# Dilated and sliding window attention with a gated unit: a half-pair order, loads by two pairs, and a ring for y

## The chip, the cores and the metric

One core of a Trainium2 chip runs the whole program. The time is the device time of the core in microseconds (us), from several executions; beside the timed runs there is one profiled execution, whose trace gives every other time here. TensorE (PE in the profile, PEld for its weight loads) multiplies matrices, VectorE (DVE) and ScalarE (ACT) do the elementwise work, GpSimd (POOL) converts inputs, SyncE (SP) issues the loads.

## The reference

For 8 batches, 8 heads, 576 positions and a head dimension of 64, attention is computed under a causal mask: heads 0 to 3 see the last 32 positions ("plain" here), heads 4 to 7 every fourth of the last 128 ("dilated"). The result, with the heads side by side as 512 channels, goes through a gated unit: a causal depthwise convolution of five taps gives the gate, a matrix gives the value, and a second matrix the output.

```python
scores = scale * np.matmul(q, k.transpose(0, 1, 3, 2))
rel = pos[:, None] - pos[None, :]
mask_plain = (rel >= 0) & (rel < window)                       # window = 32
mask_dil = (rel >= 0) & (rel < window * dilation) & (rel % dilation == 0)   # dilation = 4
...
attn = np.exp(scores); attn = attn / (np.sum(attn, axis=-1, keepdims=True) + 1e-09)
x = np.matmul(attn, v)                                          # heads side by side: (B, S, 512)
...
for k in range(K):                                              # K = 5
    gate_pre += conv_w[k][None, None, :] * xp[:, k:k + S, :]
gate = 1.0 / (1.0 + np.exp(-gate_pre))
return gate * (x @ w_val) @ w_out
```

## The kernel before, in words

**Pairs.** The work goes by head pairs: four pairs for each of eight batches, 32 in all, listed in `order` (L82). In batch 0 the dilated pairs come first; later batches go plain, dilated, plain, dilated. Positions are grouped by their remainder modulo 4, so that a dilated head becomes four heads with an ordinary window of 32 over 144 positions (96 and a rest of 48).

**One pair.** `load_qk` and `load_v` (L89, L106) issue the loads of a pair on SP, two pairs ahead in program order; four buffers of each input let them run ahead. `convert` (L132) casts on POOL: V of a dilated pair, or q and k of a plain pair (96 rows and 48 rows apart, four casts). `transpose_in` (L152) transposes q and k on TensorE into a PSUM bank; VectorE copies them to `qT` and `kT` (L182), except `kT` of a plain pair, which ScalarE copies (L179). A plain pair has four transposes of 96 rows and four of 48 for each of q and k; a dilated one six of 96.

`scores(i, hf)` (L187) does one half of the pair: matmuls into a PSUM tile `sc`, exp on ScalarE into `et` (L212), and the mask as a multiplication on VectorE (L219). `attn_v(i, hf)` (L222) multiplies the masked `et` by V and a column of ones, into the same `sc` tile; VectorE takes the reciprocal of the sums (`rec`, L251) and scales the rest into `xn` (L256). The pool `ps_s` has two such tiles (L60), so a tile is taken again two halves later, once its `xn` is done. `transpose_x` (L261) transposes `xn` on TensorE, for a dilated pair by turns of 96 and 48 rows (L269, L271), and ScalarE copies the result into `xT` (L278), the 512 channels by position.

**The gated unit.** Tokens are cut into ten groups (L283). A group has, for each block of 128 channels, a conv unit (L297: five diagonal matmuls, tanh on ScalarE) and a val unit (L310: four matmuls, then VectorE combines gate and value into `y_all`, L320), and an out unit for each 128 tokens (L326: four matmuls, a ScalarE copy to `osb`, L332, and the store, issued on ScalarE's queue, L333). Banks for these and for the transposes come from one pool of four (L61).

**The order.** Every engine works in the order in which the program emits instructions. The main loop (L447) emits, for pair i: the loads and casts of pair i+2; both scores with exp and mask; `fill`; `attn_v(i, 0)`; the input transposes of pair i+1; `attn_v(i, 1)`; `fill`; `transpose_x(i)`. `fill` (L432) takes units from a queue while a budget lasts, 3.2 a pair in two shares; a conv costs 1.1, a val or out 0.9. A group enters the queue when its last batch's attention is done; so batch 0 has no units beside it, batches 1 to 6 have twelve each (the group of the batch before), and what the last batch leaves is done at the end (L472): 1024 tokens' worth, in groups of 448, 320 and 256.

The weights are loaded through POOL's queue in pairs 0 and 2 (L454, L456); the diagonal matrices of the convolution are made on VectorE after each of the first four pairs (L401).

Of the kernel before, what the change touches and what calls it, by code (L numbers as in the profile page):

```python
# [24 lines left out]
def kernel(  # L25
# [30 lines left out]
    inbuf = ctx.enter_context(tc.tile_pool(name="inbuf", bufs=4))  # L56
# [10 lines left out]
    NKT_, NVP, NVD, NET = 3, 3, 2, 4  # L67
    kTs = [consts.tile([128, 640], BF16, name=f"kT{i}") for i in range(NKT_)]
    ets = [consts.tile([128, 2, 384], BF16, name=f"et{i}") for i in range(NET)]
    vps = [consts.tile([128, NT, 2, D + 1], FP32, name=f"vp{i}") for i in range(NVP)]  # L70
# [3 lines left out]
    y_all = consts.tile([128, NCH, NTOK], BF16, name="y_all")  # L74
# [7 lines left out]
    order = [(b, g) for b in range(B) for g in ((2, 3, 0, 1) if b == 0 else (0, 2, 1, 3))]  # L82
    nat = {}
    cnt = {"p": 0, "d": 0}
# [4 lines left out]
    def load_qk(i):  # L89
        b, g = order[i]  # L90
        t = {}
        for name, src in (("q", q), ("k", k)):
            rows = src[b, 2 * g:2 * g + 2].rearrange("h (p r) d -> p h (r d)", r=R)
            a = inbuf.tile([P0, 2, R * D], FP32, name=f"{name}a")
            nc.sync.dma_start(out=a, in_=rows[0:P0])
            if is_dil(i):
                z = inbuf.tile([2 * P1, R * D], FP32, name=f"{name}zd")
                for hh in range(2):
                    nc.sync.dma_start(out=z[hh * P1:(hh + 1) * P1], in_=rows[P0:TT, hh, :])
            else:  # L100
                z = inbuf.tile([P1, 2, R * D], FP32, name=f"{name}zp")
                nc.sync.dma_start(out=z, in_=rows[P0:TT])
            t[name] = (a, z)
        nat[i] = t

    def load_v(i):  # L106
        b, g = order[i]
        t = nat[i]
        if g >= NG // 2:
            rows = v[b, 2 * g:2 * g + 2].rearrange("h (p r) d -> p h (r d)", r=R)  # L110
            a = inbuf.tile([96, 2, R * D], FP32, name="va")
            nc.sync.dma_start(out=a, in_=rows[0:96])
            z = inbuf.tile([80, 2, R * D], FP32, name="vz")
            nc.sync.dma_start(out=z, in_=rows[64:144])
            j = cnt["d"] % NVD
            cnt["d"] += 1
            t["v"] = (a, z, vd0[j], vd1[j])
        else:
            vt = vps[cnt["p"] % NVP]
            cnt["p"] += 1  # L120
            vv = v[b, 2 * g:2 * g + 2]
            nc.sync.dma_start(out=vt[:, 0, :, 0:D],
                              in_=vv[:, 0:128, :].rearrange("h p d -> p h d"))
            for hh in range(2):
                nc.sync.dma_start(
                    out=vt[:, 1:NT, hh, 0:D],
                    in_=bass.AP(tensor=v.tensor,
                                offset=v.offset + ((b * H + 2 * g + hh) * S + 64) * D,
                                ap=[[D, 128], [96 * D, NT - 1], [1, D]]))
            t["v"] = (vt,)  # L130

    def convert(i):  # L132
        if is_dil(i):
            a, z, c0, c1 = nat[i]["v"]
            for src, dst in ((a, c0), (z, c1)):
                nc.gpsimd.tensor_copy(  # L136
                    dst[:, :, :, 0:D], src.rearrange("p h (r d) -> p h r d", r=R))
        else:
            for name in ("q", "k"):
                res = []  # L140
                for src, n, x in zip(nat[i][name], (P0, P1), "az"):
                    c = work.tile([n, R, 2, D], BF16, name=f"{name}c{x}")
                    nc.gpsimd.tensor_copy(
                        c.rearrange("p r h d -> p h r d"),
                        src.rearrange("p h (r d) -> p h r d", r=R))
                    res.append(c)
                nat[i][name] = tuple(res)
# [4 lines left out]
    def transpose_in(i, name):  # L152
        a, z = nat[i][name]
        ps = bank(BF16)
        if is_dil(i):
            av, zv = hi_bf16(a), hi_bf16(z)
            pv = ps[:, 0:S].rearrange("p (f h t) -> p f h t", f=2, h=2)
            for f in range(2):
                cols = slice(f * 128, f * 128 + 128)
                for hh in range(2):  # L160
                    nc.tensor.transpose(out=pv[:, f, hh, 0:P0], in_=av[:, hh, cols],
                                        identity=ident_b[0:P0, 0:P0])
                nc.tensor.transpose(out=pv[:, f, :, P0:TT], in_=zv[:, cols],  # L163
                                    identity=ident_b[0:2 * P1, 0:2 * P1])
        else:
            for r in range(R):
                nc.tensor.transpose(out=ps[:, r * TT:r * TT + P0],
                                    in_=a[:, r, :, :].rearrange("p h d -> p (h d)"),
                                    identity=ident_b[0:P0, 0:P0])
            for r in range(R):  # L170
                nc.tensor.transpose(out=ps[:, r * TT + P0:(r + 1) * TT],  # L171
                                    in_=z[:, r, :, :].rearrange("p h d -> p (h d)"),
                                    identity=ident_b[0:P1, 0:P1])
        if name == "k":
            dst = kTs[i % NKT_]
        else:
            dst = work.tile([128, S], BF16, name="qT")
        if name == "k" and not is_dil(i):
            nc.scalar.copy(out=dst[:, 0:S].rearrange("p (t r) -> p t r", r=R),  # L179
                           in_=ps[:, 0:S].rearrange("p (r t) -> p t r", r=R))  # L180
        else:
            nc.vector.tensor_copy(dst[:, 0:S], ps[:, 0:S])  # L182
        nat[i][name + "T"] = dst
# [3 lines left out]
    def scores(i, hf):  # L187
        b, g = order[i]
        dil = g >= NG // 2
        qT, kT = nat[i]["qT"], nat[i]["kT"]  # L190
# [8 lines left out]
        if dil:  # L199
            for hh in range(2):  # L200
                o = (2 * hf + hh) * TT
                mm(hh * 96, 96, kT[:, o:o + 128], qT[:, o:o + 96])
            for hh in range(2):
                o = (2 * hf + hh) * TT
                mm(192 + hh * 48, 48, kT[:, o + 64:o + 192], qT[:, o + 96:o + TT])
        else:
            for c in range(3):
                t = 3 * hf + c
                k0 = 0 if t == 0 else 96 * t - 32
                mm(c * 96, 96, kT[:, k0:k0 + 128], qr[:, :, 24 * t:24 * t + 24])  # L210
        et = ets[(2 * i + hf) % NET]
        nc.scalar.activation(out=et[:, :, 0:HALF], in_=ps[:, :, 0:HALF],  # L212
                             func=AF.Exp, scale=scale)
        ev = et[:, :, 0:HALF]
        if dil:
            for_mask = mask_d[:, None, :].to_broadcast([128, 2, HALF])
        else:
            for_mask = mask_p[:, hf:hf + 1, :].to_broadcast([128, 2, HALF])
        nc.vector.tensor_tensor(out=ev, in0=ev, in1=for_mask, op=ALU.mult)  # L219
        state[(i, hf)] = (ps, et)  # L220

    def attn_v(i, hf):  # L222
# [8 lines left out]
        for x in range(2):  # L231
            if dil:
                _, _, c0, c1 = nat[i]["v"]
# [9 lines left out]
            else:  # L243
                vb = hi_bf16(nat[i]["v"][0])
                for c in range(3):
                    nc.tensor.matmul(out=ps[:, x, c * DA:(c + 1) * DA],  # L246
                                     lhsT=et[:, x, c * 96:c * 96 + 128],
                                     rhs=vb[:, 3 * hf + c, x, :], start=True, stop=True)
# [12 lines left out]
    def transpose_x(i):  # L261
# [5 lines left out]
        if dil:  # L267
            for r in range(R):
                nc.tensor.transpose(out=pv[:, r, 0:96], in_=xn[:, 2 * r, :, :].rearrange("p h d -> p (h d)"),  # L269
                                    identity=ident_b[0:96, 0:96])  # L270
                nc.tensor.transpose(out=pv[:, r, 96:TT], in_=xn[0:48, 2 * r + 1, :, :].rearrange("p h d -> p (h d)"),  # L271
                                    identity=ident_b[0:48, 0:48])
        else:
            for t in range(NT):
                nc.tensor.transpose(out=pv[:, :, 24 * t:24 * t + 24], in_=xn[:, t, :, :].rearrange("p h d -> p (h d)"),
                                    identity=ident_b[0:96, 0:96])
# [3 lines left out]
        del nat[i]  # L280


    groups = [(512 * j, 512) for j in range(7)] + [(3584, 448), (4032, 320), (4352, 256)]  # L283
# [11 lines left out]
    gates = {}  # L295

# [13 lines left out]
    def val_unit(gi, c):  # L310
        t0, n = groups[gi]
        ps = bank()
        for o, col, ln in pieces(t0, n):
# [5 lines left out]
        gate = gates.pop((gi, c))  # L319
        nc.vector.scalar_tensor_tensor(  # L320
            out=y_all[:, c, t0:t0 + n], in0=gate[:, 0:n], scalar=1.0, in1=ps[:, 0:n],
# [4 lines left out]
    def out_unit(t0, n):  # L326
        ps = bank()
        for c in range(NCH):
            nc.tensor.matmul(out=ps[0:n, :], lhsT=y_all[:, c, t0:t0 + n],  # L329
# [6 lines left out]
    load_qk(0)  # L336
    load_v(0)
# [22 lines left out]
    for x in kTs:  # L360
        nc.vector.memset(x[:, S:640], 0.0)
    for x in ets:
        nc.vector.memset(x[:, :, HALF:384], 1.0)
    for x in vps:
        nc.vector.memset(x[:, :, :, D:D + 1], 1.0 - 2.0 ** -9)
    convert(0)

    load_qk(1)
    load_v(1)
# [6 lines left out]
    band(mp[:, 0, 0, :, :], 0, [[1, R], [4, 24]], 1, W)  # L376
    band(mp[:, 1, 0, :, :], 32, [[1, R], [4, 24]], 1, W)
# [29 lines left out]
    COST = {"C": 1.1, "V": 0.9, "O": 0.9}  # L407
    done_tok = [0]

    def add_group(gi):  # L410
# [93 lines left out]
```

## Time and profile before

| | us |
|---|---|
| timed runs | 226.98, 231.23, 345.96 |
| median of the runs | 231.23 |
| the profiled execution's own time | 225.51 |
| its span, first to last instruction | 223.8 |
| TensorE busy | 189.1 |
| VectorE busy | 128.4 |
| ScalarE busy | 108.7 |
| GpSimd busy | 65.0 |
| first conv unit starts | 31.96 |
| last pair's attention ends, only gated units remain | 195.4 |

A line of a group or a timeline reads: source line, engine, operation, output <- input, partitions by elements. In a timeline the first column is the start in us from the beginning of the span, the second the duration; brackets hold the idle time before it, and what ended it. Matmuls are pipelined: the starts of consecutive ones are nearer than their durations, of which some 0.2 us is the way through the array. DMA moved 41.82 MB, 30.95 of them on SP's queue; 219 GB/s from 10 to 20 us, 225 and 227 in two steady batches.

### The profile page before, as it was taken

The numbers are of one execution on the slowest core, as the hardware profiler recorded it, in microseconds if no ns is written. First come the engines' busy times: TensorE is split into PE (matmuls) and PEld (weight loads), VectorE is DVE, ScalarE is ACT, GpSimd is POOL, SyncE is SP. The second block draws the span as 40 slices with busy tenths as digits, with TensorE's granted clock in tenths as the row PEclk, the third lists the DMA queues.
The fourth block names the chain that finished last, engine by engine and source line by source line (L and its number), as shares of the span: only waits on it lengthen the run. The fifth ranks groups of instructions, "written<-read, shape, count | busy, mean of one in ns | idle before, by whom it ended". The sixth has DMA issues, their size and how long they took to land.

```text
span 223.8 us, 5850 instructions
## 1 busy us (share of the span) xinstructions
PE 189.1 (85%) x2279; PEld 127.0 (57%) x2292; DVE 128.4 (57%) x311; ACT 108.7 (49%) x190; POOL 65.0 (29%) x123
## 2 busy tenths in 40 slices
PE   2666689878988898898898898889888988999992
PEld 0544545545655576556775686558655666454670
DVE  2566664775667556663666659656776566532320
ACT  2234444356554655475544753465536654643442
POOL 4296506420516150524146024602360200000000
PEclk9999999999999999996999999999999999999999
DMA  5799999747779799869989779778986300221232
GB/s 144 240 220 207 236 216 225 211 120 232 213 212 231 234 254 224 217 222 258 233 192 243 234 217 237 181 244 227 232 213 212 118 3 0 99 91 47 100 141 94
DMA packets 58757, 41.82 MB, mean 187 GB/s; under 512 B 29029, under 2 KB 54117, under 8 KB 58730
## 3 DMA queue, kind: packets, MB, share of 16 engines
q1 hardware_dynamic: 52480, 30.95, 56.1%
q10 hardware_dynamic: 5194, 9.45, 11.8%
q0 software_dynamic: 1056, 1.05, 2.9%
q8 instruction: 18, 0.29, 0.6%
q14 instruction: 9, 0.07, 0.1%
HBM read 33.04 MB, written 9.44 MB: 190 GB/s over the span
## 4 chain that ended last, share of the span: by engine, by line
PE 45%; DMA 15%; ACT 13%; DVE 10%; issue 7%; SPq 6%; ACTq 2%; POOL 0%; DVEq 0%
PE bank L303 16%; ACT et L212 9%; PE bank L315 8%; PE bank L329 5%; DVE et L219 4%; ACT osb L332 4%; DMA qa<-in_q_dram 4%; DVE xn L256 4%; DMA vp<-in_v_dram 3%; PE bank L269 3%; PE sc L246 2%; PE bank L271 2%; DMA ka<-in_k_dram 2%; ACTq L333 2%; DMA kzd<-in_k_dram 2%
## 5 line engine op out<-in xcount | busy, mean ns | idle before, releaser
L303 PE MATMUL bank<-xT,conv_diag 128*128 128x320 bf16 (+7 forms) x319 | 46.3, 295 | 0.3 <-DMA kzd<-in_k_dram 0.3
L256 DVE TENSOR_TENSOR xn<-sc,rec 96x512 bf16<-96x512 f32 (+1 forms) x64 | 39.7, 620 | 2.2
L212 ACT ACTIVATE et<-sc 128x576 bf16<-128x576 f32 x64 | 38.5, 660 | 4.8 <-PE sc L197 4.8
L307 ACT ACTIVATE gate<-bank 128x512 bf16<-128x512 f32 (+3 forms) x40 | 22.0, 556 | 32.8 <-PE bank L303 32.8
L315 PE MATMUL bank<-xT,w_val_b 128*128 128x320 bf16 (+7 forms) x254 | 37.1, 285 | 0.3 <-issue 0.3
L136 POOL CAST vda<-va 96x512 bf16<-96x512 f32 x16 | 10.0, 622 | 92.9 <-DMA va<-in_v_dram 79.3
L332 ACT ACTIVATE osb<-bank 128x512 f32<-128x512 f32 x36 | 21.6, 601 | 29.4 <-PE bank L329 23.4
L320 DVE SCALAR_TENSOR_TENSOR y_all<-gate,bank 128x512 bf16<-128x512 bf16 (+3 forms) x40 | 25.1, 628 | 18.0 <-PE bank L315 9.1
L303 PEld LDWEIGHTS <-conv_diag 128*128 128x128 bf16 x320 | 27.8, 100 | 12.6 <-issue 1.4
L329 PE MATMUL bank<-w_out_b,y_all 128*128 128x512 bf16 x134 | 33.7, 380 | 0.8 <-DVE y_all L320 0.2
L219 DVE TENSOR_TENSOR et<-et,mask_d 128x576 bf16<-128x576 bf16 x32 | 16.7, 524 | 27.9 <-ACT et L212 26.9
L278 ACT COPY xT<-bank 128x576 bf16<-128x576 bf16 x32 | 20.4, 637 | 23.1 <-PE bank L271 17.8
L219 DVE TENSOR_TENSOR et<-et,mask_p 128x576 bf16<-128x576 bf16 x32 | 16.8, 532 | 25.6 <-ACT et L212 24.6
L315 PEld LDWEIGHTS <-w_val_b 128*128 128x128 bf16 x256 | 20.8, 97 | 8.1
L329 PEld LDWEIGHTS <-y_all 128*128 128x128 bf16 x144 | 12.8, 98 | 14.4 <-DVE y_all L320 1.8
L179 ACT COPY kT<-bank 128x576 bf16<-128x576 bf16 x16 | 10.2, 638 | 20.4 <-PE bank L171 16.4
L236 PE MATMUL sc<-vda,et 96*128 96x65 bf16 x128 | 12.2, 203 | 7.6 <-DVE et L219 3.7
L246 PE MATMUL sc<-vp,et 128*128 128x65 bf16 x192 | 12.1, 201 | 7.5 <-DVE et L219 4.2
L269 PE MATMUL bank<-ident_b,xn 96*128 96x96 bf16 x64 | 14.1, 221 | 4.4 <-DVE xn L256 4.4
L251 DVE RECIPROCAL rec<-sc 96x8 f32<-96x8 f32 (+1 forms) x64 | 12.2, 191 | 9.5 <-PE sc L246 7.7
L182 DVE COPY qT<-bank 128x576 bf16<-128x576 bf16 x32 | 14.2, 444 | 3.3 <-PE bank L163 3.0
L236 PEld LDWEIGHTS <-et 96*128 96x128 bf16 x128 | 8.1, 100 | 14.1 <-DVE et L219 13.6
(62 smaller groups left out, 243.5 us busy)
## 6 DMA issues: line engine op xcount, KB each, us to landing
out_dram<-osb ACTq DMA_DIRECT2D x36, 256.0 KB, 2.3
qa<-in_q_dram SPq DMA_DIRECT2D x32, 192.0 KB, 4.1
ka<-in_k_dram SPq DMA_DIRECT2D x32, 192.0 KB, 3.4
vp<-in_v_dram SPq DMA_DIRECT2D x32, 160.0 KB, 3.8
va<-in_v_dram SPq DMA_DIRECT2D x16, 192.0 KB, 3.6
vz<-in_v_dram SPq DMA_DIRECT2D x16, 160.0 KB, 3.8
qzd<-in_q_dram SPq DMA_DIRECT2D x32, 48.0 KB, 3.4
kzd<-in_k_dram SPq DMA_DIRECT2D x32, 48.0 KB, 3.1
```

Of the source, the lines that this page charges most:

```text
L212: nc.scalar.activation(out=et[:, :, 0:HALF], in_=ps[:, :, 0:HALF], func=AF.Exp, scale=scale)
L219: nc.vector.tensor_tensor(out=ev, in0=ev, in1=for_mask, op=ALU.mult)
L236: nc.tensor.matmul(out=ps[:, x, hh * DA:(hh + 1) * DA], lhsT=et[0:96, x, hh * 96:hh * 96 + 128], rhs=c0[:, hh, r, :], start=True, stop=True)
L256: nc.vector.tensor_tensor(out=xo, in0=av[:, :, :, 0:D], in1=rec[:, :, 0:n, None].to_broadcast([96, 2, n, D]), op=ALU.mult)
L269: nc.tensor.transpose(out=pv[:, r, 0:96], in_=xn[:, 2 * r, :, :].rearrange("p h d -> p (h d)"), identity=ident_b[0:96, 0:96])
L278: nc.scalar.copy(out=xT[:, g, c0:c0 + S].rearrange("p (t r) -> p t r", r=R), in_=pv.rearrange("p r t -> p t r"))
L303: nc.tensor.matmul(out=ps[:, o:o + ln], lhsT=conv_diag[:, c, kk, :], rhs=xT[:, c, s:s + ln], start=(kk == 0), stop=(kk == K - 1))
L307: nc.scalar.activation(out=gate[:, 0:n], in_=ps[:, 0:n], func=AF.Tanh, scale=0.5)
L315: nc.tensor.matmul(out=ps[:, o:o + ln], lhsT=w_val_b[:, mc, c * 128:(c + 1) * 128], rhs=xT[:, mc, col:col + ln], start=(mc == 0), stop=(mc ...
L320: nc.vector.scalar_tensor_tensor(out=y_all[:, c, t0:t0 + n], in0=gate[:, 0:n], scalar=1.0, in1=ps[:, 0:n], op0=ALU.add, op1=ALU.mult)
L329: nc.tensor.matmul(out=ps[0:n, :], lhsT=y_all[:, c, t0:t0 + n], rhs=w_out_b[:, c, :], start=(c == 0), stop=(c == NCH - 1))
L332: nc.scalar.activation(out=osb[0:n, :], in_=ps[0:n, :], func=AF.Copy, scale=0.5)
```

## The change

The dilated pairs come first in every batch, and the loop runs by half pairs j = 0 to 63. Step j emits: at an even j the loads of two pairs (every second pair) and the casts of pair i+2; the scores and exp of half j+1; at an even j the output transposes of pair i-1 and the input transposes of pair i+1; `fill`; the mask of half j+1; `attn_v` of half j; `fill`. The pool of score tiles still has two.

Loads come by units of two pairs (four heads), with three buffers for q and k, two for the rest. The 48-row rests of q and k of a plain pair lie in one tile of 96 rows, so a plain pair has three casts and twelve input transposes of 96 rows; `kT` is then copied by ScalarE in two pieces. The dilated output transposes go four of 96, then four of 48. The first 32 columns of the plain keys are zeros, so that every key block starts at 96t. V of a plain unit is one load with one column of ones per block.

`fill` gets what is left of the planned units divided by the steps left, from step 9 on, split 0.6 and 0.4. The last three groups are 384, 384 and 256 tokens; what remains for the end are 640 tokens' worth. `y` is a ring of three tiles, one for each group.

```diff
-    inbuf = ctx.enter_context(tc.tile_pool(name="inbuf", bufs=4))
+    inbuf = ctx.enter_context(tc.tile_pool(name="inbuf", bufs=2))
...
+    units = [(b, d) for b in range(B) for d in (1, 0)]
+    order = [(b, 2 * d + e) for b, d in units for e in range(2)]
...
+    def load_unit(u, parts):
...
+            t[name] = inbuf.tile([P0, 4, R * D], FP32, name=f"{name}a", bufs=3)
...
+        for e in range(0, 2, step):
+            hl, hn = 2 * e, 2 * step
+            for n, (name, src) in enumerate((("q", q), ("k", k))):
+                rows = src[b, hs].rearrange("h (p r) d -> p h (r d)", r=R)
+                nc.sync.dma_start(out=t[name][:, hl:hl + hn], in_=rows[0:P0, hl:hl + hn])
...
     def convert(i):
...
+            for name in ("k", "q", "z"):
+                n = 2 * P1 if name == "z" else P0
+                c = work.tile([n, R, 2, D], BF16, name=f"{name}c")
...
+        for r in range(R):
+            o = r * TT + P0
+            step = S + r * P1 - o
+            pa = pq[:, o:o + P1]
+            dst = bass.AP(tensor=pa.tensor, offset=pa.offset,
+                          ap=[pa.ap[0], [step, 2], [1, P1]])
+            nc.tensor.transpose(out=dst, in_=flat(cz[:, r]), identity=ident)
+        nc.vector.tensor_copy(qT, pq[:, 0:S])
+        for lo, hi, src in ((0, P0, pk[:, 0:R * P0]), (P0, TT, pq[:, S:S + R * P1])):
+            nc.scalar.copy(
+                out=kT[:, R * lo:R * hi].rearrange("p (t r) -> p t r", r=R),
+                in_=src.rearrange("p (r t) -> p t r", r=R))
...
+    def masks(i, hf):
+        et = state[(i, hf)][1]
...
+        nc.vector.tensor_tensor(out=ev, in0=ev, in1=m, op=ALU.mult)
...
             for r in range(R):
-                nc.tensor.transpose(out=pv[:, r, 0:96], in_=xn[:, 2 * r, :, :].rearrange("p h d -> p (h d)"),
+                nc.tensor.transpose(out=pv[:, r, 0:96], in_=flat(xn[:, 2 * r]),
                                     identity=ident_b[0:96, 0:96])
-                nc.tensor.transpose(out=pv[:, r, 96:TT], in_=xn[0:48, 2 * r + 1, :, :].rearrange("p h d -> p (h d)"),
+            for r in range(R):
+                nc.tensor.transpose(out=pv[:, r, 96:TT], in_=flat(xn[0:48, 2 * r + 1]),
                                     identity=ident_b[0:48, 0:48])
...
-    groups = [(512 * j, 512) for j in range(7)] + [(3584, 448), (4032, 320), (4352, 256)]
+    groups = [(512 * j, 512) for j in range(7)] + [(3584, 384), (3968, 384), (4352, 256)]
...
+        if c == 0:
+            ys[gi] = moe_sb.tile([128, NCH, 512], BF16, name="y", bufs=3)
...
+    first_fill = 2 * NG + 1
+    left = [todo, 2 * n_steps - first_fill]
...
+    transpose_in(0)
+    scores(0, 0)
+    masks(0, 0)
+    for j in range(2 * n_steps):
+        i, hf = j // 2, j % 2
         b, g = order[i]
...
+        if hf == 0:
+            if i % 2 == 0 and i // 2 + 2 < len(units):
+                load_unit(i // 2 + 2, 1)
+            if i + 2 < n_steps:
+                convert(i + 2)
...
+        share = max(0.0, left[0]) / max(1, left[1]) if j >= first_fill else 0.0
...
+        if j + 1 < 2 * n_steps:
+            scores((j + 1) // 2, (j + 1) % 2)
+        if hf == 0:
+            if i > 0:
+                transpose_x(i - 1)
+            if i + 1 < n_steps:
+                transpose_in(i + 1)
+        fill(share * 0.6)
+        if hf == 0 and i > 0 and i % NG == 0:
+            queue.extend(ready_after.get(order[i - 1][0], []))
+        if j + 1 < 2 * n_steps:
+            masks((j + 1) // 2, (j + 1) % 2)
+        attn_v(i, hf)
+        fill(share * 0.4)
+        if hf == 1 and i < NCH:
+            conv_consts(i)
+    transpose_x(n_steps - 1)
+    queue.extend(ready_after[B - 1])
     while queue:
         run_item()
```

## The prediction

> **What bounds the kernel now.** I read the page first (engines, slices, chain of waits), then the windows by batch, then the timeline of one batch on TensorE, VectorE and ScalarE, then who waited for whom.
>
> ```profile
> span 223.8 us, 5850 instructions
> PE 189.1 (85%) x2279; PEld 127.0 (57%) x2292; DVE 128.4 (57%) x311; ACT 108.7 (49%) x190; POOL 65.0 (29%) x123
> ...
> PEclk9999999999999999996999999999999999999999
> ```
>
> TensorE leads with 85%, and one slice (from 100.7 us) shows a lower granted clock. The windows below are two steady batches (four head pairs each) and the tail; their columns are length, busy time and count of PE, PEld, DVE, ACT, POOL, then clock, DMA share, GB/s.
>
> ```profile
> 55.50:78.95 23.45, 20.95 (x286) 13.25 (x286) 14.85 (x34) 12.67 (x22) 8.30 (x13) 1.00 0.79 225
> 78.95:102.05 23.10, 20.92 (x285) 14.17 (x286) 14.31 (x34) 12.67 (x22) 8.39 (x15) 1.00 0.87 227
> 102.05:126.90 24.85, 22.68 (x285) 16.29 (x285) 14.98 (x34) 12.78 (x22) 8.98 (x15) 0.93 0.94 240
> ...
> 195.40:223.80 28.40, 23.82 (x146) 13.85 (x146) 7.35 (x15) 11.19 (x22) 0.00 (x0) 1.00 0.25 93
> ```
>
> A batch is 23.45 us; PE's 20.95 includes about 0.2 us of modelled drain per burst, so I count starts: the batch from 55.5 has gaps of 0.8, 1.1, 0.3, 1.1 and 0.7 us, 4 in all, and PE's own need is 19.4. So a batch is bound by PE, plus the places where PE catches up with VectorE or ScalarE:
>
> ```profile
> 86.82 0.24 PE L236 MATMUL sc<-vda,et 96*128 96x65 bf16 x2 [0.66 <-ACT et L212]
> ...
> 90.26 0.21 PE L269 MATMUL bank<-ident_b,xn 96*128 96x96 bf16 x1
> 90.40 0.19 PE L271 MATMUL bank<-ident_b,xn 48*128 48x48 bf16 x1
> 90.52 0.22 PE L269 MATMUL bank<-ident_b,xn 96*128 96x96 bf16 x1
> 90.67 0.19 PE L271 MATMUL bank<-ident_b,xn 48*128 48x48 bf16 x1
> ...
> 101.62 0.22 PE L269 MATMUL bank<-ident_b,xn 96*128 96x96 bf16 x1 [0.57 <-DVE xn L256]
> ```
>
> The reader sees the two stalls that the change aims at (attention times V waiting for the mask, transposes waiting for `xn`), and alternating heights at 0.13 us a transpose. VectorE in the same batch:
>
> ```profile
> 86.31 1.00 DVE L219 TENSOR_TENSOR et<-et,mask_d 128x576 bf16<-128x576 bf16 x2 [1.60 <-ACT et L212]
> 87.22 0.68 DVE L320 SCALAR_TENSOR_TENSOR y_all<-gate,bank 128x512 bf16<-128x512 bf16 x1
> 87.82 0.20 DVE L251 RECIPROCAL rec<-sc 96x8 f32<-96x8 f32 x1
> 88.05 0.69 DVE L256 TENSOR_TENSOR xn<-sc,rec 96x512 bf16<-96x512 f32 x1
> 88.66 0.44 DVE L182 COPY qT<-bank 128x576 bf16<-128x576 bf16 x1
> ```
>
> VectorE idles 1.5 to 2.1 us once per pair before the first mask, waiting for scores and exp; both halves share that wait.
>
> **The change on TensorE.** Plain input transposes fall from 16 to 12 and keep one height: four groups of heights took 63.62 to 64.59 = 0.97, twelve of 96 rows took 58.25 to 58.75 = 0.50 (the dilated ones). Grouped dilated output transposes: eight took 90.26 to 91.22 = 0.96; four of 96 then four of 48 took 63.62 to 64.11 = 0.49. Both save 0.47, two of each a batch: 1.9 us a batch, 15 us in eight if PE set the pace.
>
> **The change in the order.** The PSUM ring for scores keeps two buffers. Half j's scores, exp input and attention output share one; so scores(j+2) wait for `xn`(j). In the instruction order of the changed kernel VectorE has mask(j+1), then rec(j), then `xn`(j), and the second half's scores on PE do wait for VectorE, though their `kT` is older. Mask(j+1) needs exp(j+1), that needs scores(j+1), and these waited for `xn`(j-1). So the halves form one serial loop: what was one scores-exp wait a pair becomes two, and queued behind mask(j+1) are rec and `xn` of a half whose PE work is done; scores(j+2), and all PE work after them, wait for these.
>
> Links of the loop: `xn` end to PE 0.05 (from 78.47 to 78.52 in the chain); scores start to exp start 0.39 (16 took 0.37 of starts, so 8 take 0.19, plus 0.2 to the end of a matmul; the slower first pair, 6.89 to 7.35, bounds it at 0.46, the 0.19 of starts from below); exp start to mask start 0.70 (79.71 to 80.40, 85.60 to 86.31); mask to the next op 0.40; rec to `xn` 0.23; `xn` 0.69 or 0.55. **A second-half step** is 0.05+0.39+0.70+0.40+0.23+0.62 = 2.39. **A first-half step** has the transposes too. On PE: scores 0.19, output transposes 0.35 (plain) or 0.55 (0.49 and a change of height), input transposes 0.50. VectorE has `qT`, and for a dilated pair `kT`, ahead of mask(j+1). Dilated next: `qT` at 1.0, `kT` at 1.45, mask 1.82, rec 2.22, `xn` 2.45, next scores at 3.12. Plain next: `qT` needs the last transpose, 1.35+0.2 = 1.55; mask 1.92, `xn` 2.55, scores 3.22. Bare batch: 4x2.39 + 2x3.12 + 2x3.22 = 22.2.
>
> **The gated units in it.** A batch still carries 12 units. Conv takes 1.15 on PE (2.30 for two), val 0.87, out 0.87. Following the fill's budget line by line places them; batch 3 (half-steps 24 to 31) as an example:
> - 24: a conv after attention, hidden in PE's wait: 3.2.
> - 25: conv before attention, rec ready at 1.75 against 1.48: 2.7.
> - 26: attention behind transposes and conv, rec at 2.87 against 2.32: 3.85.
> - 27: as 25: 2.7.
> - 28: val before attention. Its y (0.62) stands ahead of mask(j+1) on VectorE and is ready at 2.4, so mask 3.0, `xn` 3.65: 4.25.
> - 29: outs hidden: 2.35.
> - 30, 31: exp stands behind the osb copy (0.60) and DMA issue (0.34) of 29 and 30 on ScalarE, until 1.05 instead of 0.39: 3.1 and 3.0.
>
> Sum 25.2. The other batches differ by where a val lands before a mask; two vals there in batch 6 make 28. I take 25.7 for batches 1 to 6. Bounds of the additions: nothing (22.2), and 5.3 with two more such vals a batch (27.5). This takes 3.5 because the delays are queue order, not shares of busy time. PE's need of 17.7 (19.4-1.9, and 0.2 for splitting the scores) is no longer the limit.
>
> **Start.** First scores stay at 6.9. In before the first conv starts at 31.96. Bare steps give 6.9+22.2 = 29 for half-step 8. The input transposes now stand ahead of attention on PE, so a late load holds attention too. Pair 1 lands at 10.1 as before, which puts half-step 1 at 12.1; pair 2's casts stand on POOL behind the mask building (15.0+3x0.61), so its `qT` comes at 17, half-step 3 at 19, 4 at 21.5, 6 at 27.2. Its transposes need pair 4's q and k: at 219 GB/s the first four pairs (3.9 MB) end near 19.5, w_val's 1 MB takes 5, 1.2 MB more lands at 30. Half-step 7 then starts at 32, 8 at 34.5; bounds 29, and 36 with half of the four conv_diag blocks (0.93 each) outside the waits.
>
> **Last batch and tail.** 23 units in eight half-steps: PE 23x0.96 + 6.1 (17.7 less a batch's 11.6 of units) = 28.2; placed step by step like batch 3, 30.5. The tail shrinks from 1024 tokens to 640: 195.4 to 219.3 is 23.3 ns a token, so 14.9, and 1.1 for the last `xT` copy that its first conv needs. Drain 219.3 to 223.8 = 4.5.
>
> **Sum.** 34.5 + 6x25.7 + 30.5 + 16 + 4.5 = 239.7 span; the profiled execution's own time is 1.7 above its span: 241.4. The nearest timed run, 226.98, is 1.5 above the profiled 225.51 (the median 5.7): 243.
>
> **At nothing.** SP issues fall from 240 to 113: loads are buffered three units ahead, and at 25.7 us a batch needs 5.05 MB, 197 GB/s, under the 225 seen; without that cover, 5.05 MB at 219 is 23.1 a batch, still shorter. POOL's 16 fewer casts (0.62): POOL waited 92.9 for loads. `kT` in two ScalarE copies costs 0.14 more (384 and 192 elements on the line through 0.60 for 512 and 0.38 for 256), done at 2.2 before 3.2. The y ring of three: its group left two batches ago. If ScalarE's cover goes, each plain step grows by what `kT` is late.
>
> **Clock.** The window from 102.05 has a clock of 0.93: 0.07 of its 24.85 us, 3.4 us at half. It follows 3.2 us in which PE had only transposes and attention (the last out matmuls ended at 98.8), and was 1.4 us longer than the batch from 55.50. In the new order half-steps 30 to 32 leave about 4.5 us without a gated unit in each batch. Such a window costs 0 to 1.7 us; I take 0 for the time, as PE waits anyway, and 1.7 a batch for the upper end. The Trainium skill, "TensorE: Matmul & The Clock Gate", section "What's actually happening", says that one idle window of about 3.4 us halves the clock, against this change; by it, an estimate of seven windows would add 12 us, to 255.
>
> **Rivals.** (1) The order of VectorE's queue, above: 243; chance 0.72. For it: order and loop. Against it: the additions are placed by hand. (2) The units hide in the loop's waits: the total is 88.7 + 6P for a batch period P (34.5+30.5+16+4.5+3.2 = 88.7); P half way, 23.7 or less, gives 231 and below, no change; chance 0.11. (3) Faster: the PE savings reach the end because the loop is shorter than PE's work. Place: mask to `xn`; it decides below P = 22, under the bare 22.2; at PE's 17.7 the time is 195, at 21.5 it is 218. For it: the 4 us of gaps and 1.9 saved; against: the order of mask and rec. Chance 0.07. (4) Half clock in each batch on top: 255; chance 0.10.
>
> The range goes from 229 (P = 23.4) to 256 (rival 4). A change within 2% is about what a measurement of this kernel cannot tell from none; faster 0.07, same 0.10 (rival 2 but for 0.01), slower 0.83.
>
> **What would show it.** Steady batches near 25.7; second-half steps 2.4 to 3, first-half 3.1 to 4.3; PE waits before the scores released by VectorE's `xn`, instead of before attention; VectorE idle before nearly every mask (64, not 31); PE's share near 75%; output transposes at half their length; a tail of 640 tokens. It is wrong if scores start without waiting for `xn`, if rec runs well after the mask ended, or if loads end the waits after 40 us.

## The result and the profile after

The changed kernel takes 257.78 us (median of four runs, 256.12 to 260.1), the kernel before 230.14 (median of four, 226.98 to 345.96). The ratio is 1.128 with a 95% interval of 1.109 to 1.147: slower by an eighth. Here and below a ratio compares only the runs within 1.5% of the fastest of their kernel, which leaves out 231.23 and 345.96 of before and 260.1 of after. The profiled execution took 256.71 us, its span 255.0.

From the page of the changed kernel:

```profile
span 255.0 us, 5579 instructions
...
PE 192.4 (75%) x2264; PEld 127.8 (50%) x2264; DVE 129.7 (51%) x314; ACT 114.0 (45%) x206; POOL 54.6 (21%) x109
...
PEclk9999999977999999999799979995899979999999
```

TensorE's busy time is 3 us more than before although 64 transposes (four in each of 16 plain pairs) and most height changes are gone; its share fell from 85% to 75%. The clock row has seven slices below 9 where it had one. It counts only time for which the trace has a record of the clock; the first record stands at 47.09 us (33.75 before). That TensorE ran at half speed ahead of it is read from its matmuls, here five of 512 columns on either side:

```profile
44.26 2.32 PE L329 MATMUL bank<-xT,conv_diag 128*128 128x512 bf16 x5
49.06 1.24 PE L329 MATMUL bank<-xT,conv_diag 128*128 128x512 bf16 x5
```

I mark a half-step by the start of its scores. The windows below run from half-step 8 to 16, 16 to 24 and so on (batches 1 to 6), then batch 7, then the tail; columns as in the prediction.

```profile
37.30:70.07 32.77, 26.23 (x241) 14.29 (x242) 16.34 (x39) 13.44 (x24) 9.39 (x16) 0.90 1.03 195
70.07:95.99 25.92, 19.91 (x276) 12.41 (x277) 14.69 (x34) 13.41 (x24) 5.74 (x10) 1.00 0.96 227
95.99:121.50 25.51, 19.91 (x276) 13.23 (x276) 16.09 (x34) 13.41 (x24) 7.24 (x12) 1.00 1.03 238
121.50:148.61 27.11, 21.41 (x276) 15.49 (x277) 14.82 (x34) 13.39 (x24) 6.28 (x10) 0.94 0.91 213
148.61:173.95 25.34, 21.55 (x276) 15.60 (x278) 14.81 (x34) 13.30 (x24) 6.02 (x10) 0.92 0.88 196
173.95:204.24 30.29, 22.66 (x276) 16.30 (x277) 14.50 (x34) 13.33 (x24) 4.74 (x8) 0.89 0.22 59
204.24:235.05 30.81, 29.11 (x304) 18.25 (x305) 15.68 (x35) 15.64 (x29) 0.00 (x0) 0.95 0.11 39
235.05:255.00 19.95, 15.12 (x135) 10.09 (x133) 3.90 (x8) 7.46 (x15) 0.00 (x0) 1.00 0.28 102
```

A batch at full clock takes 25.5 to 25.9 us, where it took 23.1 to 23.5; the batches with a clock of 0.89 and 0.90 take 30 and 33; the 0.90 of batch 1 leaves out its first 9.8 us, also at half clock. VectorE does the same work as before, ScalarE about 0.7 us more a batch.

Who holds TensorE now, from the waits of the changed kernel (us in total, times, longest):

```profile
PE sc L219 <- DVE xn L280: 46.6, 39, 2.3
PE bank L180 <- DMA qa<-in_q_dram: 3.8, 2, 3.4
```

Before, none of TensorE's waits was above 4.4 us in total:

```profile
PE bank L269 <- DVE xn L256: 4.4, 8, 0.6
PE bank L161 <- DMA qa<-in_q_dram: 3.4, 1, 3.4
```

Now the scores wait 46.6 us for `xn`, and the wait for loads is about what it was. VectorE in half-steps 24 and 25 shows how:

```profile
97.69 0.84 DVE L244 TENSOR_TENSOR et<-et,mask_d 128x576 bf16<-128x576 bf16 x1
98.45 0.19 DVE L275 RECIPROCAL rec<-sc 96x8 f32<-96x8 f32 x1
98.68 0.69 DVE L280 TENSOR_TENSOR xn<-sc,rec 96x512 bf16<-96x512 f32 x1
100.46 0.46 DVE L244 TENSOR_TENSOR et<-et,mask_d 128x576 bf16<-128x576 bf16 x1 [1.09 <-ACT et L233]
```

and TensorE beside it:

```profile
95.99 0.31 PE L219 MATMUL sc<-qT,kT 64*128 64x96 bf16 x8 [2.34 <-DVE xn L280]
...
97.19 0.23 PE L264 MATMUL sc<-vdb,et 80*128 80x65 bf16 x2
...
99.42 0.31 PE L219 MATMUL sc<-qT,kT 64*128 64x96 bf16 x8 [0.91 <-DVE xn L280]
```

The attention matmuls of half 24 end at 97.42; their `rec` runs at 98.45, as soon as the mask of half 25 is through. `xn` ends at 99.37, the next scores start at 99.42, and VectorE then sits 1.09 us until exp has gone through ScalarE. That is the serial loop of the prediction, link by link.

### The profile page after: what moved, and what is told of

Its sections match the earlier page's. It is cut to its first block, busy times and chain, and to the rows that moved or that the text cites. A ratio compares the mean times of both kernels' runs of the same rounds, so it can differ in the third digit from the quotient of the medians.

```text
span 255.0 us, 5579 instructions
## 1 busy us (share of the span) xinstructions
PE 192.4 (75%) x2264; PEld 127.8 (50%) x2264; DVE 129.7 (51%) x314; ACT 114.0 (45%) x206; POOL 54.6 (21%) x109
## 4 chain that ended last, share of the span: by engine, by line
PE 55%; DVE 25%; ACT 7%; issue 4%; SPq 3%; DMA 3%; ACTq 2%; POOL 1%; DVEq 0%
PE bank L329 16%; DVE xn L280 11%; PE bank L358 9%; PE bank L341 8%; PE sc L219 7%; DVE et L244 5%; DVE y L348 4%; ACT osb L361 3%; DMA ka<-in_k_dram 3%; ACT et L233 3%; DVE rec L275 3%; PE bank L300 2%; PE bank L180 2%; PE bank L293 2%; PE bank L189 2%
## 5 line engine op out<-in xcount | busy, mean ns | idle before, releaser
L233 ACT ACTIVATE et<-sc 128x576 bf16<-128x576 f32 x64 | 41.5, 650 | 75.7 <-PE sc L219 72.4
L219 PE MATMUL sc<-qT,kT 64*128 64x96 bf16 x448 | 21.3, 214 | 49.3 <-DVE xn L280 46.6
L329 PE MATMUL bank<-xT,conv_diag 128*128 128x384 bf16 (+7 forms) x340 | 53.3, 307 | 1.1 <-ACT xT L303 1.1
L219 PEld LDWEIGHTS <-kT 64*128 64x128 bf16 x448 | 13.0, 102 | 66.8 <-DVE xn L280 48.7
L348 DVE SCALAR_TENSOR_TENSOR y<-gate,bank 128x512 bf16<-128x512 bf16 (+2 forms) x40 | 25.3, 633 | 30.7 <-PE bank L341 25.9
L333 ACT ACTIVATE gate<-bank 128x512 bf16<-128x512 f32 (+2 forms) x40 | 22.0, 555 | 35.7 <-PE bank L329 35.2
L358 PE MATMUL bank<-w_out_b,y 128*128 128x512 bf16 x144 | 36.7, 380 | 0.4 <-DVE y L348 0.2
L329 PEld LDWEIGHTS <-conv_diag 128*128 128x128 bf16 x340 | 29.4, 105 | 14.0 <-issue 4.5
L358 PEld LDWEIGHTS <-y 128*128 128x128 bf16 x144 | 12.2, 97 | 13.4 <-DVE y L348 3.4
L203 ACT COPY kT<-bank 128x384 bf16<-128x384 bf16 (+1 forms) x32 | 12.9, 408 | 3.7 <-DVE qT L201 2.2
```

Source lines behind the costliest of these rows:

```text
L219: nc.tensor.matmul(out=ps[:, x, out_c:out_c + ln], lhsT=lhs[rb], rhs=rhs[rb], start=True, stop=True)
L329: nc.tensor.matmul(out=ps[:, o:o + ln], lhsT=conv_diag[:, c, kk, :], rhs=xT[:, c, s:s + ln], start=(kk == 0), stop=(kk == K - 1))
L333: nc.scalar.activation(out=gate[:, 0:n], in_=ps[:, 0:n], func=AF.Tanh, scale=0.5)
L348: nc.vector.scalar_tensor_tensor(out=ys[gi][:, c, 0:n], in0=gate[:, 0:n], scalar=1.0, in1=ps[:, 0:n], op0=ALU.add, op1=ALU.mult)
L358: nc.tensor.matmul(out=ps[0:n, :], lhsT=ys[gi][:, c, o:o + n], rhs=w_out_b[:, c, :], start=(c == 0), stop=(c == NCH - 1))
```

## The experiments

Each kernel's time stands with its ratio to the kernel before, run on the same chip (228.65 us for the first four, 230.13 for the next four, 229.25 for the last). The changed kernel itself has 1.128.

**e1: the next mask behind `xn`.**

```diff
-        if j + 1 < 2 * n_steps:
-            masks((j + 1) // 2, (j + 1) % 2)
         attn_v(i, hf)
+        if j + 1 < 2 * n_steps:
+            masks((j + 1) // 2, (j + 1) % 2)
         fill(share * 0.4)
```

> The changed kernel, with one move: the mask of half j+1 is emitted behind the attention times V, rec and xn of half j, instead of ahead of them. The theory of the serial loop (scores wait for xn two halves back, xn stands behind the next mask, and this mask behind exp and the scores) says that the loop opens: rec and xn run as soon as their attention matmuls are done. Batches 2 to 5 fall from 25.3 to 27.1 us to about 20 (TensorE's own need of 17.7 and some waits), the first batch by 3 to 4, the whole to 200 to 215 us. Rival 1, the half clock as the cause and not its consequence: the order of two operations on VectorE changes little, 245 us or more. Rival 2, the loads by two pairs: nothing changes, 256.

Measured: 237.32 us, ratio 1.038 (1.027 to 1.048). One move of one VectorE operation takes back about 20 of the 28 us. Batches 2 to 5 take 23.84, 22.98, 25.19 and 23.20; the second half-steps without a unit fall from 2.2 to 2.9 us to 1.6 to 2.0. So the order of VectorE's queue is a cause, and rivals 1 and 2 of the expectation fail. The 20 us are not the order's alone: the profile has one stretch of half clock behind the start instead of five. In batches 2 and 3, at full clock in both kernels, the move is worth 2.1 and 2.5 us. And 200 to 215 was wrong: scores still wait 30.5 us for `xn`. That wait, and then VectorE and TensorE of this kernel in half-step 27:

```profile
PE sc L219 <- DVE xn L280: 30.5, 38, 1.7
```

```profile
96.63 0.20 DVE L275 RECIPROCAL rec<-sc 96x8 f32<-96x8 f32 x1 [0.79 <-PE sc L264]
96.86 0.69 DVE L280 TENSOR_TENSOR xn<-sc,rec 96x512 bf16<-96x512 f32 x1
97.47 0.45 DVE L244 TENSOR_TENSOR et<-et,mask_p 128x576 bf16<-128x576 bf16 x1
```

```profile
96.36 0.23 PE L264 MATMUL sc<-vdb,et 80*128 80x65 bf16 x2
97.61 0.30 PE L219 MATMUL sc<-qT,kT 64*128 64x96 bf16 x6 [1.02 <-DVE xn L280]
```

`rec` now follows attention at once, yet the scores two halves on still need this `xn`, 1.0 us after attention. Where no unit was placed behind attention, TensorE has nothing to do in that time.

**e2: TensorE kept busy.** The added matmuls use the identity and a mask as operands; their result is not used.

```diff
+    def warm(n):
+        ps = bank()
+        for _ in range(n):
+            nc.tensor.matmul(out=ps[:, 0:288], lhsT=ident_b, rhs=mask_d,
+                             start=True, stop=True)
+
     def run_item():
+        ran[0] += 1
...
         fill(share * 0.4)
+        if ran[0] == 0:
+            warm(8)
+        ran[0] = 0
```

`ran` counts the units of a half-step, so `warm` runs where there was none.

> The changed kernel, with eight additional matmuls (288 columns, result unused) at the end of every half-step that has no gated unit, where TensorE waits for xn. They add no operation to any other engine. If the 15 us by which the forecast was short are the halved clock of TensorE (to 47.1 us from the start, 53.9 to 60.7, and five windows later), the clock stays up through most of these and the time falls to 240 to 247 us. If the long batches 1 and 6 come from how the units are bunched in their steps, the time stays at 255 to 259. If the added matmuls themselves delay the scores, it rises above 260.

Measured: 246.81 us, ratio 1.080 (1.070 to 1.090): 11 us less for more work on TensorE. Three of its batches (1, 5 and 6):

```profile
35.69:64.53 28.84, 23.02 (x244) 13.11 (x250) 15.80 (x39) 13.30 (x24) 9.85 (x16) 0.88 1.17 226
...
143.43:167.83 24.40, 20.96 (x282) 15.35 (x285) 14.76 (x34) 13.41 (x24) 6.02 (x10) 1.00 0.84 201
167.83:195.91 28.08, 21.83 (x291) 15.80 (x293) 14.43 (x34) 13.40 (x24) 4.74 (x8) 1.00 0.24 64
```

The halved clock is most of the miss: it now ends at 14.1 us instead of 47.1, and later stretches of it come to 13.7 us instead of 23.9. Batch 2, at full clock in both kernels, takes 25.92 in both. Batch 6 stays at 28.08 at full clock: there the units are bunched, two ahead of attention in two half-steps. Batch 1 still has a clock of 0.88.

**e3: the transposes alone, in the order of before.** The edit to the kernel before is that of the change's `transpose_x` and of `zp`, `convert` and the plain `transpose_in`; the core is

```diff
             for r in range(R):
                 nc.tensor.transpose(out=pv[:, r, 0:96], in_=xn[:, 2 * r, :, :].rearrange("p h d -> p (h d)"),
                                     identity=ident_b[0:96, 0:96])
+            for r in range(R):
                 nc.tensor.transpose(out=pv[:, r, 96:TT], in_=xn[0:48, 2 * r + 1, :, :].rearrange("p h d -> p (h d)"),
```

> The kernel before with the transposes of the change alone: a plain pair's 48-row rests of q and k in one tile (three casts, twelve transposes of 96 rows, kT in two copies), and the dilated output transposes four of 96 and then four of 48. Order, loads and units stay. If TensorE sets the pace of the kernel before, 1.9 us a batch come off most of it: 10 to 15 us less, 212 to 220 us. If the waits for mask and xn grow by what TensorE gains, 225 to 230.

Measured: 222.23 us, ratio 0.972 (0.961 to 0.982), 6 us less than before and short of the 10 to 15 expected; its profile had the clock at half in three stretches against one before. Two full-clock batches take 22.62 and 23.07. The part of the change that removes work is a gain by itself.

**e4: the loads cut into pairs again.**

```diff
-                load_unit(i // 2 + 2, 1)
+                load_unit(i // 2 + 2, 2)
...
-    load_unit(1, 1)
+    load_unit(1, 2)
```

> The changed kernel with every load cut into pairs again (V of plain pairs excepted), order and all else as it is. If loads are hidden but for the start, where the casts of pair 2 waited 2.2 us for the first k of the second unit, the time falls by 0 to 3 us: 254 to 258. If the larger loads cost more than that, by landing late (8 us instead of 4), it falls by 5 or more, to 252 or less.

Measured: 257.60 us, ratio 1.131 (1.121 to 1.140): no difference. Half-step 8 starts at 34.35 instead of 37.30, as the first k of the second unit lands sooner; the 3 us are lost later, in a profile with more of the half clock (mean 0.933 against 0.953). The larger loads are not the cause of the eighth; e9 below agrees.

**e5: three score tiles.**

```diff
-    ps_s = ctx.enter_context(tc.tile_pool(name="ps_s", bufs=2, space=bass.MemoryType.PSUM))
-    ps_m = ctx.enter_context(tc.tile_pool(name="ps_m", bufs=4, space=bass.MemoryType.PSUM))
+    ps_s = ctx.enter_context(tc.tile_pool(name="ps_s", bufs=3, space=bass.MemoryType.PSUM))
+    ps_m = ctx.enter_context(tc.tile_pool(name="ps_m", bufs=2, space=bass.MemoryType.PSUM))
```

> The changed kernel with three score tiles instead of two, and two banks instead of four for transposes and units (PSUM holds no more). Order as it is. If the ring of two is the link that makes the halves wait for each other, scores are no longer released by xn: TensorE's waits for xn (46.6 us in the changed kernel) fall under 10, and scores run a half further ahead. What two banks cost is open: with banks enough, 215 to 235 us; if each unit waits for the copy of the one before the last, 240 to 260, with the waits named after those copies. If the order on VectorE alone makes the loop, the waits for xn stay.

Measured: 261.35 us, ratio 1.139 (1.127 to 1.151). TensorE's longest waits in this kernel, and that of the scores for `xn`:

```profile
PE bank L300 <- DVE xn L280: 11.7, 12, 2.5
PE bank L192 <- ACT xT L303: 6.0, 13, 1.3
PE bank L293 <- DVE xn L280: 5.8, 8, 1.5
...
PE sc L219 <- DVE xn L280: 1.6, 6, 0.3
```

The scores' wait for `xn` falls from 46.6 to 1.6 us; the output transposes wait now, which really need it, and banks wait for ScalarE's copies. In batch 3 the half-step without a unit, 31, falls from 2.88 to 0.54 us, and the first ones take 4.28 to 7.38, the longest in part at half clock. By the waits, the ring is the other link of the loop. The time cannot price it: two banks bring waits of their own, and half clock behind the start grows from 23.9 to 37.5 us in this profile.

**e6: dilated output transposes ungrouped in the new order.** The second `for r in range(R):` of `transpose_x` is taken out of the changed kernel.

> The changed kernel with the dilated output transposes by turns of 96 and 48 rows again, 0.47 us more of TensorE for each of 16 pairs. They stand ahead of the input transposes, which qT and then the mask on VectorE wait for. If the loop theory holds, their time is on the loop in the first half-steps: 16 x 0.47 = 7.5 us, 263 to 267. If TensorE has room there, 256 to 259.

Measured: 267.69 us, ratio 1.168 (1.158 to 1.179), 10 us more. Half-steps 26 and 28 go from 3.86 and 4.20 to 4.47 and 4.82, 0.61 and 0.62 more. In half-step 26 the eight transposes take 1.10 us by turns (106.42 to 107.52) and 0.47 grouped (102.45 to 102.92): 0.63, not the 0.47 expected, and 16 times that is the 10 us. TensorE's time ahead of the input transposes is on the loop, although TensorE idles a quarter of the span.

**e7: the mask ahead of the first units.**

```diff
+        if j + 1 < 2 * n_steps:
+            masks((j + 1) // 2, (j + 1) % 2)
         fill(share * 0.6)
...
-        if j + 1 < 2 * n_steps:
-            masks((j + 1) // 2, (j + 1) % 2)
```

> The changed kernel with the mask of half j+1 emitted ahead of the first units of the step, so that no y of a val stands ahead of it on VectorE. The loop stays. By the forecast's placing, a step with a val ahead of attention loses about 0.4 us (y still stands ahead of rec): some 12 such steps, 4 to 6 us less, 251 to 254. If VectorE's queue matters little, 256 to 259.

Measured: 250.55 us, ratio 1.090 (1.078 to 1.102), 7 us less, a little under the 251 to 254 expected. Half-step 28 goes from 4.20 to 3.83, 44 from 4.27 to 3.83; half-step 49, with a conv and a val ahead, from 5.31 to 4.00. The clock has a part in the 7 us: stretches of half clock behind the start come to 17.1 us instead of 23.9.

**e8: a version from the findings.** The kernel of e3, with the output transposes behind the next scores and a budget that lasts for all four pairs.

```diff
-    per = 3.2
+    per = 2.9
...
         scores(i, 0)
         scores(i, 1)
+        if i > 0:
+            transpose_x(i - 1)
+            if i % NG == 0:
+                for gi in group_ready.get(order[i - 1][0], []):
+                    add_group(gi)
         fill(per * 0.35)
...
         fill(per * 0.65)
-        transpose_x(i)
```

> The kernel before with the grouped transposes, and two moves more: the output transposes of pair i-1 go behind the scores of pair i, where TensorE waited for the mask (0.66 and 1.1 us), and the budget is 2.9 a pair instead of 3.2, so that the fourth pair has units too where TensorE waited for xn. If TensorE's waits of 4 us a batch are what stands between 21.8 and its own need of 17.5, a batch falls to about 20 and the time to 205 to 214 us. If the waits only move, 218 to 224.

Measured: 215.14 us, ratio 0.939 (0.930 to 0.948). It beats both kernels. Two steady batches:

```profile
64.18:86.13 21.95, 19.20 (x278) 12.63 (x278) 14.79 (x34) 12.60 (x24) 6.22 (x10) 1.00 0.88 242
86.13:108.00 21.87, 19.39 (x279) 13.58 (x279) 14.84 (x35) 12.62 (x24) 6.60 (x12) 1.00 0.84 233
```

A batch is 22 us, not 20, so the expected waits went in part only, and the time is just above the 205 to 214 expected. The clock stays full from 34 us to the end of the work, where e3 lost it three times, so what each of the two moves is worth by itself is not shown.

**e9: e2 and e4 together.**

> The changed kernel with both: eight additional matmuls (result unused) at the end of each half-step without a unit, and the loads cut into pairs. Alone the first took 11 us off, the second brought half-step 8 forward by 3.0 us, which half-clock windows ate up later. If these two are the whole miss of the forecast, together they give its 243 us, 241 to 246, with half-step 8 near 33 and steady batches at 25 to 26. If the loads by pair cost something in the steady batches, the time stays at 246 to 249.

Measured: 246.73 us, ratio 1.077 (1.065 to 1.088): as e2 alone. Half-step 8 starts at 33.0, but batches 1 and 6 take 29.2 and 29.7. Both still hold half clock (45.8 to 52.6 and 175.5 to 178.9), so this run does not show what would be left without any.

## Why the prediction was right and wrong, point by point

**Direction and mechanism: right.** The serial loop over `xn`, mask, exp and scores set the pace: the trace shows it link by link, taking out the queue order shortened the time (e1), and taking out the ring ended the scores' wait for `xn` (e5), though not the time. Batch 3, placed by hand, was 3.2, 2.7, 3.85, 2.7, 4.25, 2.35, 3.1, 3.0; measured 3.43, 2.78, 3.86, 2.77, 4.20, 2.34, 3.24, 2.88. Rivals 2 and 3 are out: no batch came under 25.3, and 23.7 was the point. One sign failed: VectorE was to idle before nearly every mask; it waited for exp before 25 of the 64 (31 waits before), and in the first half-steps its wait stands ahead of `qT` instead (32 times), where the prediction's own placing of a first half-step has it.

**Time: wrong, by 14.8 us, and outside the range by 1.8.** The terms of the sum, on the span:

| term | predicted | measured |
|---|---|---|
| to half-step 8 | 34.5 | 37.3 |
| batches 1 to 6 | 154.2 | 166.9 |
| batch 7 | 30.5 | 30.8 |
| tail | 16 | 15.6 |
| drain | 4.5 | 4.4 |
| span | 239.7 | 255.0 |

The step that failed is the clock's term, "I take 0 for the time, as PE waits anyway". The runs showed this in its place: TensorE was at half clock to 47.1 us and in five stretches later, 23.9 us of them, and keeping it busy (e2) gave back 11 us of the miss. PE does not only wait: its units and transposes stand on the loop (in e6, 0.63 us more of transposes lengthened a half-step by 0.61), so a half clock lengthens the loop. Full-clock batches 2 and 3 are within 0.2 of 25.7; the excess of 12.7 sits in batch 1 (+7.1, with 16.6 of its 32.8 us at half clock), batch 6 (+4.6) and batch 4 (+1.4).

The rival that came closest is the fourth, half clock on top of the loop, at 255, to which I gave 0.10. The 23.9 us are its seven windows of 3.41, but that the numbers agree is in part luck: two windows lie in batch 1 and two about the start of batch 6, batches 2 and 3 have none, and part of batch 6's excess is the placing of units. The Trainium skill, "TensorE: Matmul & The Clock Gate", section "What's actually happening", by which the prediction estimated 12 us for seven windows, says that the clock halves after an idle window of about 3.4 us. This trace agrees on the length, but the windows ahead of the five falls were not idle: TensorE was busy for 18 to 45% of them (last section).

Two smaller sizes were off. Batch 6 was placed at 28, then averaged away in 25.7: at full clock it took 28.1 (e2). And the start took 2.8 more: the first k of the second unit came late (17.26 instead of 15.0 on GpSimd), and first half-steps at the slow start clock (4 and 6) took 3.90 and 3.87 where I had 3.1 to 3.2; at the full clock of e9 they took 3.09 and 3.21, and with loads by pair alone (e4) half-step 8 started at 34.35. A third was small in itself: the 0.47 us saved by grouping eight transposes, read from plain input transposes, is 0.63 for the output ones in the new order (e6).

**Costs set at nothing.** Larger loads and fewer SP issues: right for the time as a whole (e4). The fewer casts, `kT` in two copies and the y ring were not taken out by any run. The shorter transposes were in the sum, as links of the first half-steps, and rightly: in the new order undoing the dilated half costs 10 us (e6), in the order of before all of them give 6 (e3). The gain is inside the 257.78, covered by the loop's loss.

**Open.** Batch 1 lost the clock in every half-pair kernel except e1 and e5 (between 45.8 and 62.1 us, also with added matmuls). About 4 us of the miss, in batches 1 and 6 of e9, are not told apart between clock and bunched units. No run has the new queue order, three score tiles and banks enough together, so what is left of the loop after e1 has no price of its own.

## What to carry to other kernels

Issuing the next step's scores early brought nothing here while a ring of two tiles made them wait for the step's last operation: follow one tile round its ring, through every in-order queue, and add up the links; that sum is the period, whatever the busy shares say. Within a queue, put the operation that frees a buffer ahead of the one that has just become possible; here that one swap was worth 20 us in all, 2 to 2.5 of them in each batch at full clock in both kernels. When a change makes the leading engine idle, price its clock too, and test the parts of a large change alone: one part here was a gain that the others hid.

## What the runs showed of the hardware

After its first record, the clock of the changed kernel changes only at multiples of 3.41 us, and falls to half five times, for 3.41 or 6.83 us. These are the windows of 3.41 us just ahead of the five falls, then the two least busy ones that were followed by full clock (start and end, length, busy time of PE and the others):

```profile
50.50:53.91 3.41, 1.52 (x18) 0.87 (x18) 1.92 (x5) 1.09 (x2) 0.61 (x1) 1.00 1.11 189
118.77:122.18 3.41, 1.14 (x33) 0.93 (x30) 1.11 (x3) 1.39 (x3) 0.00 (x0) 1.00 0.91 229
146.08:149.49 3.41, 1.49 (x37) 1.29 (x38) 1.35 (x4) 1.25 (x3) 0.00 (x0) 1.00 0.76 228
169.97:173.38 3.41, 1.48 (x24) 0.87 (x21) 2.16 (x8) 2.01 (x4) 0.00 (x0) 1.00 0.41 154
200.69:204.10 3.41, 0.61 (x14) 0.44 (x14) 2.25 (x7) 0.65 (x1) 0.00 (x0) 1.00 0.00 1
...
135.83:139.25 3.42, 1.61 (x28) 1.37 (x27) 2.17 (x5) 1.34 (x4) 1.48 (x2) 1.00 1.12 231
180.21:183.62 3.41, 1.64 (x22) 1.36 (x20) 1.88 (x4) 0.60 (x1) 1.69 (x3) 1.00 0.00 0
```

TensorE was busy for 18 to 45% of the five, and for 47% or more of every other window at full clock. It is the same in the eleven traces together, cut at their own changes of clock: all 21 full-clock windows under 47% were followed by half clock, 14 of the 25 from 47 to 57%, and 5 of the 545 above (one of them the fall of the kernel before, at 82%). Of 54 windows at half clock 40 were followed by full clock, and TensorE was busy for at least 81% of each of these. So these kernels lose the clock where TensorE is busy for about half of a window or less, and winning it back takes much more. Why those five busier windows were followed by half clock stays open.

A mask on VectorE takes 0.45 to 0.46 us, but 0.70 on the mean when a GpSimd cast runs at the same time (14 of the changed kernel's 64 masks; 0.84 at 97.69 above, during the cast that started at 97.61). This lies on the loop as well: in e2 the same mask took 0.45 us, and half-step 24 took 3.04 us instead of 3.43.
